# Interleaving the first two query passes by halves of the keys, and adding causal masks on TensorE instead of selecting on GpSimd, in a two-part attention kernel

## Chip, cores, metric

One core of one Trainium2 chip. The metric is the device time of one execution in microseconds, as the median of several executions. Below, PE is TensorE, ACT is ScalarE, DVE is VectorE, POOL is GpSimd. All runs compared here are of the fast state. One profile is one execution.

## The reference, cut to what matters

```python
def _A_ref(x, wqkv, wo):                      # S = 2048, D = 448, H = 16, Dh = 28
    ...
    scores = jnp.einsum('bhqd,bhkd->bhqk', q, k) * Dh ** (-0.5)
    p = _softmax(scores, axis=-1)             # full attention, no mask
    o = jnp.einsum('bhqk,bhkd->bhqd', p, v)
    ...
def _B_ref(x, wq, wk, wv, wo, beta):          # four segments of 512, causal within each
    ...
    for s in range(N):
        logits = jnp.einsum('bhqd,bhkd->bhqk', qs, ks) * scale + mask
        p = _softmax(logits, axis=-1)
        a_dot = jnp.einsum('bhqk,bhkd->bhqd', p, vs)
        ... # plus a linear-attention memory of the segments before, mixed in by sigmoid(beta)
```

Part A has 1024 banks of scores (I call a bank the scores of 128 keys by 512 queries for one head). Part B, of which only the causal blocks are computed and packed, has 160.

## The kernel before

Each bank needs an exp. Most go through ACT, in units of alternately three and two banks, with one PSUM buffer for each size, so that PE can write the scores of one unit while ACT reads the other. Some banks of part A ("DVE banks") go through a polynomial exp on DVE instead. There the `fraction` step runs on POOL if POOL is free, else on DVE.

The instructions of every engine are issued in an order that the kernel's Python plans with a model of the engines' times (`m["dve"]`, `m["pool"]` and so on). The model decides how many banks go to DVE. It adds zero "filler" matmuls (`fill`) where PE's recent load is below a limit; in that load each matmul's columns count by the share of the array that its tile covers.

The causal masks of part B before the change, after the exp, on POOL, with what the model charges for them:

```python
def emit_scores():                            # cut
    ...                                       # scores of the unit's banks into ps (PE)
    nc.scalar.activation(out=pt[:, 0:n, :], in_=ps[:, 0:n, :], func=ACT.Exp, scale=scale)
    e = on_act(n * CW, True, e)
    eff.append(e)
    ...
    while offs:                               # the diagonal blocks of the unit
        ...
        nc.gpsimd.affine_select(out=blk, in_=blk, compare_op=ALU.is_ge, fill=0.0,
                                base=0, pattern=pat, channel_multiplier=-1)
        p0 = max(m["pool"], e + SEM)
        m["pool"] = p0 + 260 + k * P          # POOL is taken: a fraction may go to DVE
        masks.append((p0, m["pool"]))         # DVE is charged 0.8 of each overlap with this
        e = m["pool"] + 30
        offs = offs[k:]
    ...                                       # then the products with V may be issued
```

```python
# the DVE exp of two banks: the fraction step
if m["pool"] > got + POOLQ:
    step(got, 267 * n, lambda: fraction(nc.vector), after_z)
    return
fraction(nc.gpsimd)
p0 = max(m["pool"], got)
m["pool"] = p0 + 160 + n * 595
masks.append((p0, m["pool"]))
```

The kernel keeps three more banks in PSUM, the "ring", for projections, DVE banks and the accumulators of the products with V. An accumulator holds its slot for a whole query pass of one head group. Before the change pass after pass is done; the projections and transposes of all of part A's keys for the first head group come ahead of everything else, and DVE takes no bank until they are nearly done.

The softmax here doesn't subtract the row's maximum and nothing guards it: scores larger than these inputs give would overflow.

Of the kernel before, what the change touches and what calls it, by code (L numbers as in the profile page):

```python
# [10 lines left out]
ALU = mybir.AluOpType  # L11
# [49 lines left out]
LASTV = 18  # L61
POOLQ = 300
HOLD = 0


@with_exitstack
def kernel(
# [126 lines left out]
        mblk.append(t)  # L194
    macc = const.tile([P, G, P], FP32)

    blocks = const.tile([P, P], BF16)
    nc.gpsimd.memset(blocks[:], 0.0)
    for j in range(4):
# [77 lines left out]
    def mm(out, mode, tl, n, dep, **kw):  # L277
        rows, cols = kw["lhsT"].shape[0], kw["lhsT"].shape[1]
        e = pe_time(mode, tl, n, dep, rows * cols / (P * P))
        nc.tensor.matmul(out, **kw)  # L280
        return e
# [15 lines left out]
    def dve(ready, prio, stream, emit, then=None, gate=None, slot=None):  # L297
        seq[0] += 1
        tasks.append((ready + SEM, prio, seq[0], stream, emit, then, gate, slot))
# [21 lines left out]
    for n, (kind, a, b) in enumerate(SEQ):  # L321
        T[kind, a, b] = len(order)
        if kind == "A":
            order += [("A", a, b, kt, j) for kt in range(NT) for j in range(4)]
        else:
            order += [(bk, b, s, None, j) for bk, s in (
                ("X", 2 * a), ("Y", 2 * a), ("Z", 2 * a), ("X", 2 * a + 1), ("Y", 2 * a + 1))
                for j in range(4)]
    T_END = len(order)
    ends = [T[k] for k in SEQ[1:]] + [T_END]  # L330

# [11 lines left out]
    def diag_blocks(b):  # L343
        return {"A": [], "X": [0], "Y": [0, 3 * P], "Z": [0, 2 * P]}[b[0]]
# [53 lines left out]
    unit_left = []  # L398
    unit_pv = []
    eff = []  # L400
    st = {"u": 0, "pos": 0, "ys": 0, "es": 0, "work": 0.0, "nrm": 0, "ot": 0}
    taken = set()


# [133 lines left out]
    def emit_scores():  # L538
        u = st["u"]
        bs, pos = next_banks()  # L540
        nb = NBS[u % 2]
        dep = max(when([x for b in bs for x in score_toks(b)]), eff[u - 2] if u >= 2 else 0.0)
        ps = scp.tile([P, nb, CW], FP32, tag=f"sc{nb}", name="ps_s")
        e = 0.0
        parts = [(n, i, b, p_) for i, b in enumerate(bs) for n, p_ in enumerate(score_parts(b))]
        for n, i, b, (t, q0, o0, w) in sorted(parts, key=lambda x: x[0]):
            kind, g, s, kt, j = b
            side = "A" if kind == "A" else "B"
            rows = slice(j * HP, j * HP + DH)
            kk, qq = kT[side, g, t // 4], qT[side, g, q0 // CW]  # L550
            for x in kq_of(b, t, q0):
                kq_used(x)
            ko, qo = t % 4 * P, q0 % CW
            e = max(e, mm(ps[:, i, o0:o0 + w], "S", j, w, dep,
                          lhsT=kk[rows, ko:ko + P], rhs=qq[rows, qo:qo + w],
                          start=True, stop=True, tile_position=(j * HP, 0)))
        n = len(bs)
        if u >= 2 * PT_BUFS:
            e = max(e, unit_pv[u - 2 * PT_BUFS])
        pt = ptp.tile([P, nb, CW], BF16, tag=f"pt{nb}", name="pt")  # L560
        nc.scalar.activation(out=pt[:, 0:n, :], in_=ps[:, 0:n, :], func=ACT.Exp, scale=scale)  # L561
        e = on_act(n * CW, True, e)
        eff.append(e)
        ptf = pt[:].rearrange("p n c -> p (n c)")
        offs = [i * CW + o for i, b in enumerate(bs) for o in diag_blocks(b)]
        while offs:
            k = 1
            if len(offs) > 1:
                step = offs[1] - offs[0]
                while k < len(offs) and offs[k] - offs[k - 1] == step:  # L570
                    k += 1
            if k == 1:
                blk, pat = ptf[:, offs[0]:offs[0] + P], [[1, P]]
            else:
                base = ptf[:, offs[0]:offs[0] + P]
                blk = bass.AP(tensor=base.tensor, offset=base.offset,
                              ap=[base.ap[0], [step, k], [1, P]])
                pat = [[0, k], [1, P]]
            nc.gpsimd.affine_select(out=blk, in_=blk, compare_op=ALU.is_ge, fill=0.0,  # L579
                                    base=0, pattern=pat, channel_multiplier=-1)  # L580
            p0 = max(m["pool"], e + SEM)
            m["pool"] = p0 + 260 + k * P
            masks.append((p0, m["pool"]))
            e = m["pool"] + 30
            offs = offs[k:]
        unit_left.append(sum(len(pv_parts(b)) for b in bs))
        unit_pv.append(0.0)
        for i, b in enumerate(bs):
            for part in pv_parts(b):
                pend.append([e, b, i, pt, part, u])  # L590
        st["u"] += 1
        st["pos"] = pos
        return bs
# [418 lines left out]
    def t_piece(r, half):  # L1012
        box = {}

        def atom(i, t0):
            def f(slot, dep):
                if i == 0 and t0 == 0:
                    box["ps"] = ring([P, 2, CW], BF16, "ps_t", slot)
                c = 2 * half + i
                for t in (t0, t0 + 1):  # L1020
                    e = pe_time("F", 0, P, dep)
                    nc.tensor.transpose(box["ps"][:, i, t * P:(t + 1) * P],  # L1022
                                        xnA[r][:, t, XC[c]:XC[c] + P], ident[:])
                return e
            return f

        def evac(e, slot):
            def then(e):
                slots[slot] = e
                rt["x", "A", r, half] = e  # L1030
            dve(e, 0, 533, lambda: nc.vector.tensor_copy(
                out=xT(slice(2 * half, 2 * half + 2), r * CW, (r + 1) * CW),
                in_=box["ps"][:]), then)

        return piece(0, [("xn", r)], [("F", 114, atom(i, t0)) for i in range(2) for t0 in (0, 2)],
                     evac)
# [175 lines left out]
    def spread(items, p0, p1):  # L1212
        cost = [sum(a[1] for a in it["atoms"]) + 100 for it in items]
        tot, c = sum(cost), 0.0
        for it, k in zip(items, cost):
            it["pos"] = p0 + (p1 - p0) * c / tot
            plan.append(it)
            c += k

    def q_(side, g, sc):  # L1220
        return kq_piece("q", side, g, sc)

    def k_(side, g, sc):
        return kq_piece("k", side, g, sc)

    head = [kq_piece("k", "A", 0, 0, P, 2 * P), kq_piece("k", "A", 0, 0, 2 * P, CW),
            t_piece(1, 0), t_piece(1, 1), k_("A", 0, 1),
            v_piece("A", (0, 1), 0), v_piece("A", (2, 3), 0),
            t_piece(2, 0), t_piece(2, 1), k_("A", 0, 2),
            v_piece("A", (4, 5), 0), v_piece("A", (6, 7), 0),  # L1230
            t_piece(3, 0), t_piece(3, 1), k_("A", 0, 3)]
    head += [v_piece("A", (t, t + 1), 0) for t in range(8, 16, 2)] + [q_("A", 0, 1)]
    spread(head, -100, -50)

    first = [q_("A", 0, 2), k_("A", 1, 0), q_("A", 1, 0), k_("A", 1, 1), q_("A", 1, 1),
             k_("A", 1, 2), q_("A", 1, 2), q_("A", 0, 3), k_("A", 1, 3), q_("A", 1, 3)]
# [128 lines left out]
    def fuse(bs):  # L1365
        used = {b[4] for b in bs}
        if sum(x["pos"] < 0 for x in side_work) > HEADQ:
            return
        for _ in range(2):
            if backlog(m["top"]) > BACKLOG:  # L1370
                return
            s = free_slot(m["top"])
            if s is None:
                return
            b = vbank_pick(used)
            if b is None:
                return
            emit_vbank(b, s)
            used.add(b[4])
# [42 lines left out]
    def pe_step(t):  # L1422
# [5 lines left out]
        if bs:  # L1428
            r = when([x for b in bs for x in score_toks(b)])
            if r is None:  # L1430
                force = "side"
            elif u >= 2 * PT_BUFS and unit_left[u - 2 * PT_BUFS]:
                force = "pv"
            else:
                avail = max(r, eff[u - 2] if u >= 2 else 0.0) + SEM
                deadline = m["act"] - 435
                if avail <= t + 4:
                    got = emit_scores()
                    fuse(got)
                    return  # L1440
        elif not ended and not side_work and not plan and not open_ and not tasks_left():
            fs = [i for i in range(3) if slots[i] is not None]
            if len(fs) >= 2:
                last_step(3, fs[0])
                last_step(2, fs[1])
                last_begin()
                ended.append(1)
                return
# [105 lines left out]
```

## Time and profile before

| | before |
|---|---|
| time | 510.46 us (510.23 to 510.75) |
| banks on DVE, of 1184 | 130 |
| units of three and two banks on ACT | 211 and 210, and one of a single bank |
| first exp starts, last exp ends, end | 8.3, 497.9, 508.4 us |
| DVE idle from 10 to 40 us | 15.6 us |
| DVE idle from 210 to 430 us (part B is spread over this) | 22.6 us |

The first lines of the page: the busy time of each engine, then the same in 40 slices of 12.7 us, in tenths; PEclk is the clock that TensorE was granted.

```profile
span 508.4 us, 12361 instructions
...
PE 475.4 (94%) x4918; PEld 168.6 (33%) x4918; DVE 445.7 (88%) x777; ACT 492.9 (97%) x450; POOL 144.6 (28%) x199
...
DVE  4349999999999999989989989879979958998993
...
POOL 8202211221122110351260431372161183202110
PEclk9999999999999999999999999999999999999999
```

ACT is busy wherever there is anything to do. DVE is not: its row begins with 4349, and from the 18th slice on it has sevens and eights. The costliest groups (line, engine, operation, tiles, shape and count; busy us and mean ns; idle before, and what ended it):

```profile
L561 ACT ACTIVATE pt<-ps_s 128x1536 bf16<-128x1536 f32 (+1 forms) x422 | 480.4, 1337 | 2.0 <-PE ps_s L280 1.3
...
L513 POOL TENSOR_SCALAR vz<-vy 128x1024 f16<-128x1024 uint16 x59 | 71.0, 1203 | 290.6 <-DVE vy L458 147.0
...
L579 POOL TENSOR_SCALAR_AFFINE_SELECT pt<-pt 128x256 bf16<-128x256 bf16 (+3 forms) x112 | 59.5, 559 | 54.4 <-ACT pt L561 54.3
L280 PE MATMUL acc<-warm 128*32 128x512 bf16 (+1 forms) x634 | 68.5, 384 | 0.0
```

The 112 selects take 59.5 us of POOL, the fillers 68.5 us of PE. Put in order of time, two exps start never closer than 1.330 us (three banks) or 0.903 us (two banks). I call "late starts" the sum of what the distances between consecutive exps have above that: 7.5 us. A bank on ACT therefore costs (1.330 + 0.903) / 5 = 0.447 us, and ACT leaves nothing else to gain than banks moved away, late starts and the two ends.

Two stretches of 25 us with part B in them (from and to in us, its length, then busy us and instructions of PE, PE's weight loads, DVE, ACT, POOL, then clock, DMA share and GB/s):

```profile
325.00:350.00 25.00, 22.75 (x291) 8.68 (x283) 19.76 (x41) 24.60 (x24) 16.28 (x29) 1.00 0.16 41
400.00:425.00 25.00, 22.64 (x255) 8.50 (x248) 18.29 (x37) 24.40 (x23) 15.21 (x29) 1.00 0.17 48
```

DVE has 5 to 7 us of idle in each, POOL is busy for over 15 us.

### The profile page before, as it was taken

What the parts mean: (1) busy time and instruction counts of PE and PEld (TensorE: products, weight loads), DVE (VectorE), ACT (ScalarE), POOL (GpSimd) and SP (SyncE); (2) the same over time, 40 slices, a digit from 0 to 9 for tenths busy, and PEclk for the clock granted to TensorE, in tenths of its full rate; (3) what the DMA queues carried; (4) which work ended last, traced back from release to release, by engine and by line L of the source; (5) the groups of instructions that cost most, each with busy time, mean ns of one, the idle gap of its engine ahead of it and who ended that gap; (6) DMA issues with size and microseconds to landing.
All of it is one profiled execution on the core that took longest, in us unless ns stands there. A gap on an engine that the chain in (4) does not pass through costs nothing.

```text
span 508.4 us, 12361 instructions
## 1 busy us (share of the span) xinstructions
PE 475.4 (94%) x4918; PEld 168.6 (33%) x4918; DVE 445.7 (88%) x777; ACT 492.9 (97%) x450; POOL 144.6 (28%) x199
## 2 busy tenths in 40 slices
PE   8999999999999999999889999899999999999996
PEld 5443233343332333333223333433333333333332
DVE  4349999999999999989989989879979958998993
ACT  5999999999999999999999999999999999999993
POOL 8202211221122110351260431372161183202110
PEclk9999999999999999999999999999999999999999
DMA  9200000000033100022021102012312120312112
GB/s 249 56 1 5 22 13 13 3 22 4 23 109 73 37 9 3 23 66 48 20 66 46 44 6 65 23 31 65 101 52 57 50 76 18 108 50 60 39 48 65
DMA packets 42178, 23.76 MB, mean 47 GB/s; under 512 B 22636, under 2 KB 37804, under 8 KB 42120
## 3 DMA queue, kind: packets, MB, share of 16 engines
q1 hardware_dynamic: 40808, 21.72, 16.1%
q0 software_dynamic: 416, 0.81, 0.7%
q8 instruction: 38, 0.62, 0.5%
q10 hardware_dynamic: 896, 0.45, 0.3%
q14 instruction: 20, 0.16, 0.1%
HBM read 16.58 MB, written 4.28 MB: 41 GB/s over the span
## 4 chain that ended last, share of the span: by engine, by line
ACT 52%; PE 22%; issue 19%; DVE 5%; POOL 1%; DMA 1%; DVEq 0%; ACTq 0%; POOLq 0%
ACT pt L561 50%; PE ps_s L280 6%; PE acc L280 5%; PE ps_proj L280 3%; PE ps_v L280 2%; PE ps_y L280 2%; ACT phiq L1042 1%; PE ps_kn L280 1%; PE ps_warm L219 1%; DVE vy L458 1%; DVE y L1080 1%; POOL pt L579 1%; DVE vz L505 1%; DVE oT L753 1%; PE ps_t L1022 0%
## 5 line engine op out<-in xcount | busy, mean ns | idle before, releaser
L561 ACT ACTIVATE pt<-ps_s 128x1536 bf16<-128x1536 f32 (+1 forms) x422 | 480.4, 1337 | 2.0 <-PE ps_s L280 1.3
L280 PE MATMUL ps_s<-qTA,kTA 28*128 28x512 bf16 x894 | 141.1, 383 | 20.3 <-ACT pt L561 17.4
L513 POOL TENSOR_SCALAR vz<-vy 128x1024 f16<-128x1024 uint16 x59 | 71.0, 1203 | 290.6 <-DVE vy L458 147.0
L280 PE MATMUL acc<-pt,vA 128*32 128x512 bf16 x894 | 116.8, 386 | 0.0
L280 PEld LDWEIGHTS <-kTA 28*128 28x128 bf16 x1024 | 46.4, 91 | 144.1 <-issue 140.0
L495 DVE SCALAR_TENSOR_TENSOR ve<-vy,vz 128x1024 uint16<-128x1024 int32 x65 | 80.8, 1243 | 0.1
L579 POOL TENSOR_SCALAR_AFFINE_SELECT pt<-pt 128x256 bf16<-128x256 bf16 (+3 forms) x112 | 59.5, 559 | 54.4 <-ACT pt L561 54.3
L280 PE MATMUL acc<-warm 128*32 128x512 bf16 (+1 forms) x634 | 68.5, 384 | 0.0
L506 DVE TENSOR_TENSOR vz<-vz,vl 128x1024 f16<-128x1024 f16 x65 | 50.1, 770 | 0.1
L280 PEld LDWEIGHTS <-vA 128*32 128x32 bf16 x1024 | 31.7, 94 | 47.8 <-issue 41.1
L505 DVE TENSOR_TENSOR vz<-vz 128x1024 f16<-128x1024 f16 x65 | 47.2, 726 | 0.2
L280 PE MATMUL ps_proj<-xT_100,wst 128*32 128x512 bf16 x512 | 38.3, 383 | 0.1
L280 PE MATMUL ps_proj<-xT_99,wst 128*32 128x512 bf16 (+2 forms) x512 | 37.1, 374 | 0.3 <-DVE vy L458 0.2
L280 PE MATMUL acc<-ve,vA 128*32 128x512 bf16 x130 | 33.5, 383 | 0.0
L280 PEld LDWEIGHTS <-wst 128*32 128x32 bf16 x1024 | 22.4, 95 | 28.2 <-issue 18.4
L280 PE MATMUL ps_s<-qTB,kTB 28*128 28x384 bf16 (+3 forms) x256 | 25.7, 299 | 5.0 <-ACT pt L561 4.2
L509 DVE TENSOR_SCALAR vl<-vz 128x1024 f16<-128x1024 f16 x65 | 27.3, 420 | 1.2 <-POOL vz L513 1.2
L720 DVE COPY osb<-acc 128x512 f32<-128x512 f32 x31 | 21.2, 683 | 7.0 <-PE acc L280 7.0
L280 PEld LDWEIGHTS <-warm 128*32 128x32 bf16 (+1 forms) x642 | 18.9, 94 | 21.5 <-issue 15.3
L753 DVE TENSOR_TENSOR oT<-osb,bc 128x512 bf16<-128x512 f32 x31 | 24.7, 797 | 0.0
L280 PE MATMUL acc<-pt,vB 128*32 128x128 bf16 (+3 forms) x256 | 20.5, 303 | 0.6 <-POOL pt L579 0.4
L280 PE MATMUL ps_y<-woB,oT 128*128 128x448 bf16 x80 | 20.7, 356 | 0.2
(388 smaller groups left out, 496.9 us busy)
## 6 DMA issues: line engine op xcount, KB each, us to landing
out_dram<-y SPq DMA_DIRECT2D x31, 112.0 KB
xn<-in_A_x_dram SPq DMA_DIRECT2D x3, 448.0 KB
wst<-in_A_wqkv_dram SPq DMA_DIRECT2D x2, 249.0 KB
woA<-in_A_wo_dram POOLq DMA_DIRECT2D x4, 98.0 KB, 7.2
woB<-in_B_wo_dram POOLq DMA_DIRECT2D x4, 98.0 KB, 4.5
wst<-in_A_wqkv_dram SPq DMA_DIRECT2D x1, 336.0 KB
wst<-in_B_wv_dram SPq DMA_DIRECT2D x1, 336.0 KB
wst<-in_B_wk_dram SPq DMA_DIRECT2D x1, 336.0 KB
```

What stands on the lines that cost most here:

```text
L219: nc.tensor.matmul(wps[:], lhsT=warm[:, 0:P], rhs=warm[:], start=True, stop=True)
L280: nc.tensor.matmul(out, **kw)
L458: dve(e0, 0, 533, lambda: nc.vector.tensor_scalar(out=pr["y"][:, i, :], in0=ps[:], scalar1=Y1, scalar2=Y0, op0=ALU.mult, op1=ALU.add), aft ...
L495: step(t, 533 * n, lambda: nc.vector.scalar_tensor_tensor(out=ef.bitcast(U16), in0=y, scalar=2.0 ** -9, in1=z, op0=ALU.mult, op1=ALU.add), ...
L505: step(t, 267 * n, lambda: nc.vector.tensor_mul(z, z, z), lambda t: step(t, 267 * n, lambda: nc.vector.tensor_mul(z, z, l), whole))
L506: lambda t: step(t, 267 * n, lambda: nc.vector.tensor_mul(z, z, l), whole))
L509: step(t, 133 * n, lambda: nc.vector.tensor_scalar(out=l, in0=z, scalar1=Z3, scalar2=Z2, op0=ALU.mult, op1=ALU.add), square)
L513: eng.tensor_scalar(out=z, in0=y.bitcast(U16).rearrange("p (c t) -> p c t", t=2)[:, :, 0], scalar1=2.0 ** -16, scalar2=Z0, op0=ALU.mult, o ...
L561: nc.scalar.activation(out=pt[:, 0:n, :], in_=ps[:, 0:n, :], func=ACT.Exp, scale=scale)
L579: nc.gpsimd.affine_select(out=blk, in_=blk, compare_op=ALU.is_ge, fill=0.0, base=0, pattern=pat, channel_multiplier=-1)
L720: nc.vector.tensor_copy(out=os_[0][:], in_=a[:])
L753: nc.vector.tensor_mul(get_oT(side, s)[:, g, :], os_[0][:], bc[:])
```

## The change

It has two parts. First, the order of the first two query passes is changed to first half of the keys for pass 0, first half for pass 1, second halves for both; half of the first projections can then come later, and DVE may take banks early. Second, the masks become matmuls: a triangle of -1e9 times the identity is to be added to the diagonal blocks of the scores in PSUM, before the exp, and the selects go, together with what the model charged for them.

```diff
+triu = const.tile([P, P], BF16)              # -1e9 where masked, built once on POOL
 ...
+first = order[:128]
+half = [[b for b in first if b[2] == cq and (b[3] < SPLIT) == lo] for cq in range(2)
+        for lo in (True, False)]
+order[:128] = half[0] + half[2] + half[1] + half[3]
 ...                                          # in emit_scores, after the scores:
+fuse(bs)                                     # DVE banks of this round, moved up to here
+for i, b in enumerate(bs):
+    offs = diag_blocks(b)
+    ...
+    e = max(e, mm(blk, "F", 0, k * P, 0.0, lhsT=ident[:], rhs=tri, start=False,
+                  stop=True, skip_group_check=True))
 ...                                          # after the exp:
-while offs:
-    ...
-    nc.gpsimd.affine_select(out=blk, in_=blk, ...)
-    p0 = max(m["pool"], e + SEM)
-    m["pool"] = p0 + 260 + k * P
-    masks.append((p0, m["pool"]))
-    e = m["pool"] + 30
 ...
-st = {..., "ys": 0, ...}                     # DVE's input buffers, shared with part A's x
+st = {..., "ys": 3, ...}                     # ... each counted free once its x is transposed
 ...
-head = [k, k, t(1), t(1), k1, v, v, t(2), t(2), k2, v, v, t(3), t(3), k3, v, v, v, v, q1]
+head = [k, k, t(1), t(1), v, k1, v, q1, v, v]                  # before anything else
+head = [t(2), t(2), k2, t(3), t(3), v, k3, v, v, v]            # spread over banks 8 to 72
 ...                                          # scores with masks are planned earlier:
-deadline = m["act"] - 435
+k = sum(len(diag_blocks(b)) for b in bs)
+deadline = m["act"] - 435 - (k and SWITCH + k * P / 2.4 + MLEAD)
```

(The head lists are abbreviated.)

More of the change, by code (lines that the diff above doesn't have):

```diff
@@ L63 @@
 HOLD = 0
+MLEAD = 0
+SPLIT = 8
 @with_exitstack
@@ L195 @@
     macc = const.tile([P, G, P], FP32)
+    triu = const.tile([P, P], BF16)
+    nc.gpsimd.memset(triu[:], 0.0)
+    nc.gpsimd.affine_select(out=triu[:], in_=triu[:], compare_op=ALU.is_ge, fill=-1e9,
+                            base=0, pattern=[[1, P]], channel_multiplier=-1)
     blocks = const.tile([P, P], BF16)
@@ L400 @@
     eff = []
-    st = {"u": 0, "pos": 0, "ys": 0, "es": 0, "work": 0.0, "nrm": 0, "ot": 0}
+    st = {"u": 0, "pos": 0, "ys": 3, "es": 0, "work": 0.0, "nrm": 0, "ot": 0}
     taken = set()
@@ L556, in emit_scores @@
                           start=True, stop=True, tile_position=(j * HP, 0)))
+        fuse(bs)
+        for i, b in enumerate(bs):
+            offs = diag_blocks(b)
+            if not offs:
+                continue
+            k = len(offs)
+            blk = ps[:, i, 0:P]
+            if k > 1:
+                blk = bass.AP(tensor=blk.tensor, offset=blk.offset,
+                              ap=[blk.ap[0], [offs[1], 2], [1, P]])
+            tri = triu[:] if k == 1 else bass.AP(
+                tensor=triu[:].tensor, offset=triu[:].offset,
+                ap=[triu[:].ap[0], [0, 2], [1, P]])
+            e = max(e, mm(blk, "F", 0, k * P, 0.0, lhsT=ident[:], rhs=tri, start=False,
+                          stop=True, skip_group_check=True))
         n = len(bs)
@@ L564, in emit_scores @@
         ptf = pt[:].rearrange("p n c -> p (n c)")
-        offs = [i * CW + o for i, b in enumerate(bs) for o in diag_blocks(b)]
-        while offs:
-            k = 1
-            if len(offs) > 1:
-                step = offs[1] - offs[0]
-                while k < len(offs) and offs[k] - offs[k - 1] == step:
-                    k += 1
-            if k == 1:
-                blk, pat = ptf[:, offs[0]:offs[0] + P], [[1, P]]
-            else:
-                base = ptf[:, offs[0]:offs[0] + P]
-                blk = bass.AP(tensor=base.tensor, offset=base.offset,
-                              ap=[base.ap[0], [step, k], [1, P]])
-                pat = [[0, k], [1, P]]
-            nc.gpsimd.affine_select(out=blk, in_=blk, compare_op=ALU.is_ge, fill=0.0,
-                                    base=0, pattern=pat, channel_multiplier=-1)
-            p0 = max(m["pool"], e + SEM)
-            m["pool"] = p0 + 260 + k * P
-            masks.append((p0, m["pool"]))
-            e = m["pool"] + 30
-            offs = offs[k:]
         unit_left.append(sum(len(pv_parts(b)) for b in bs))
@@ L1030, in then @@
                 rt["x", "A", r, half] = e
+                st["ys"] -= half
             dve(e, 0, 533, lambda: nc.vector.tensor_copy(
@@ L1226 @@
     head = [kq_piece("k", "A", 0, 0, P, 2 * P), kq_piece("k", "A", 0, 0, 2 * P, CW),
-            t_piece(1, 0), t_piece(1, 1), k_("A", 0, 1),
-            v_piece("A", (0, 1), 0), v_piece("A", (2, 3), 0),
-            t_piece(2, 0), t_piece(2, 1), k_("A", 0, 2),
-            v_piece("A", (4, 5), 0), v_piece("A", (6, 7), 0),
-            t_piece(3, 0), t_piece(3, 1), k_("A", 0, 3)]
-    head += [v_piece("A", (t, t + 1), 0) for t in range(8, 16, 2)] + [q_("A", 0, 1)]
+            t_piece(1, 0), t_piece(1, 1), v_piece("A", (0, 1), 0), k_("A", 0, 1),
+            v_piece("A", (2, 3), 0), q_("A", 0, 1), v_piece("A", (4, 5), 0), v_piece("A", (6, 7), 0)]
     spread(head, -100, -50)
+    head = [t_piece(2, 0), t_piece(2, 1), k_("A", 0, 2), t_piece(3, 0), t_piece(3, 1)]
+    head += [v_piece("A", (8, 9), 0), k_("A", 0, 3)]
+    head += [v_piece("A", (t, t + 1), 0) for t in range(10, 16, 2)]
+    spread(head, 8, 8 * SPLIT + 8)
     first = [q_("A", 0, 2), k_("A", 1, 0), q_("A", 1, 0), k_("A", 1, 1), q_("A", 1, 1),
@@ L1435, in pe_step @@
                 avail = max(r, eff[u - 2] if u >= 2 else 0.0) + SEM
-                deadline = m["act"] - 435
+                k = sum(len(diag_blocks(b)) for b in bs)
+                deadline = m["act"] - 435 - (k and SWITCH + k * P / 2.4 + MLEAD)
                 if avail <= t + 4:
-                    got = emit_scores()
-                    fuse(got)
+                    emit_scores()
                     return
```

## The prediction

> **What bounds it now.** ScalarE (ACT): 97% busy by the page (492.9 of 508.4 us), 480.4 of it in 422 exps of scores. In order of time, two exps start never closer than 1.330 us (three banks of 512 scores) or 0.903 us (two banks); 211 and 210 of them make 470 us. The rest of 8.3 to 497.9 us is other activations (14 us) and about 7.5 us of stalls. The head before and the 10.5 us tail after stay as they are. So time moves only (a) by 0.447 us (2.233/5) for each bank that goes to DVE instead, and (b) by ACT stalls.
>
> DVE computes 130 of 1184 banks (count of its score reads). A bank costs it 0.69 + half of (1.24 + 0.77 + 0.73 + 0.42) = 2.27 us (groups by shape). DVE is 98% busy from 40 to 200 us, but idle about 16 us between 10 and 40 us, and about 20 us in the ten-us windows from 210 to 430 us that hold part B's selects.
>
> **What the change does.**
> 1. 112 selects on POOL, 59.5 us, go. POOL is hardly on the chain (1%); PE waited for selects 0.4 us in all. DVE instructions overlapped by selects lasted only some 2 us longer in total[...]. The larger effect is indirect: the model in the kernel that orders the emission charges DVE 0.8 of each overlap with a select and sends the fraction step to DVE when POOL is late (6 times, 0.74 us each). Without that, part B should use perhaps half its 20 us of idle DVE, plus 4.4 + 2 us: some 7 more banks, -3 us.
> 2. Interleaved halves: half of the first projections is deferred, and DVE banks may start near 20 instead of 36 us. But two live accumulators leave one of three PSUM ring slots for projections and DVE banks from about 23 to 52 us: only 3 or 4 more banks, -1.5 us, and 0.3 us fewer early stalls.
> 3. Mask matmuls: 160, of 128 or 256 columns, full-array mode. By the measured spacing (0.32 us for a 512-column group with a change of mode, against 0.21) a unit gets 0.1 us for the mode plus about 0.17 (two banks) or 0.26 us (three), between scores and exp. In part B's 34 three-bank units the last score now ends at a median 0.71 us after the previous exp's start, and that exp lasts 0.903: 0.36 us more doesn't fit. Two-bank units (1.330 us) fit. Scores can start somewhat earlier, so I charge 0.05 to 0.12 us per three-bank unit: +2 to +3.5 us. [...]
>
> **Sum.** 510.5 - 3 - 1.8 + 2.5 = about 508; the re-planned schedule may save a little more: 507.0 us, 8 in 10 between 502.5 and 511.5. Faster by over 2% 0.06, within 2% 0.91, slower 0.03.
>
> **What would show it.** DVE score reads 137 to 144; exps about 5 fewer; first DVE banks before 36 us. Median start-to-start of part B's three-bank units up from 0.903 to about 0.97 us. POOL busy down by about 60 us. ACT still at 96 to 97%.
>
> **What would make it wrong.** Projections starving behind one slot, so that ACT waits for keys at 35 to 50 us (slower); masks fully hidden, or 15 more DVE banks (502); masks stalling two-bank units too (512).

## The result, and the profile after

The change runs in 507.43 us (507.17 to 507.93, 4 runs) against 510.46 us. Ratios here are the mean time of one kernel's fast runs over that of the other's in the same rounds, so they are not quite the ratios of the medians. This one is 0.9941, 95% interval 0.9924 to 0.9959: 0.6% faster, within 2%.

The same lines of the page as before, then the same groups:

```profile
span 505.8 us, 12171 instructions
...
PE 474.5 (94%) x4877; PEld 170.7 (34%) x4883; DVE 466.0 (92%) x801; ACT 490.6 (97%) x446; POOL 104.2 (21%) x100
...
DVE  4779899999999999999999989999999999999992
...
POOL 8312211111132111111212111121111021112210
PEclk9999999999999999999999999999999999999999
```

```profile
L586 ACT ACTIVATE pt<-ps_s 128x1536 bf16<-128x1536 f32 (+1 forms) x418 | 477.4, 1300 | 1.9 <-PE ps_s L286 1.1
L523 POOL TENSOR_SCALAR vz<-vy 128x1024 f16<-128x1024 uint16 x70 | 89.4, 1278 | 379.9 <-DVE vy L468 223.3
...
L286 PE MATMUL acc<-warm 128*32 128x512 bf16 (+2 forms) x429 | 47.8, 383 | 0.2
...
L286 PE MATMUL ps_s<-triu,ident 128*128 128x256 bf16 (+1 forms) x160 | 25.7, 255 | 0.0
```

POOL is 40 us less busy (not 60: eleven more fractions run there). DVE's row begins 4779 and has hardly an eight left. There are 160 mask matmuls, 25.7 us of PE. PE isn't busier for them: the fillers went down from 68.5 to 47.8 us. The two stretches with part B again:

```profile
325.00:350.00 25.00, 22.62 (x275) 9.34 (x277) 23.47 (x47) 24.73 (x24) 5.41 (x4) 1.00 0.21 58
400.00:425.00 25.00, 21.69 (x261) 9.54 (x259) 24.44 (x52) 24.81 (x23) 3.60 (x3) 1.00 0.19 52
```

DVE is busy where it was idle, and POOL is down to a third and a quarter.

Where the 2.5 us between the two profiles' spans come from, in us (before rounding the spans are 508.35 and 505.83):

| piece | before | after | difference |
|---|---|---|---|
| start to first exp | 8.3 | 8.4 | +0.1 |
| least time of the exps (units of three x 1.330 + of two x 0.903) | 470.3 | 465.8 | -4.5 |
| late starts | 7.5 | 9.4 | +2.0 |
| other activations between, and the single bank | 11.9 | 12.1 | +0.2 |
| last exp to end | 10.4 | 10.1 | -0.3 |

DVE takes 140 banks in place of 130. By time of their score reads:

| banks on DVE that start in | 0 to 60 us | 60 to 200 | 200 to 430 | after |
|---|---|---|---|---|
| before | 11 | 46 | 53 | 20 |
| after | 14 | 46 | 62 | 18 |

The first starts at 15.9 us, where it was 36.9. DVE's idle time falls from 15.6 to 7.0 us between 10 and 40 us, and from 22.6 to 9.2 us between 210 and 430 us.

The masks can be seen on PE. These are a three-bank unit of part B (start us, us, instruction):

```profile
329.79 0.40 PE L286 MATMUL ps_s<-qTB,kTB 28*128 28x384 bf16 x6 [0.25 <-ACT pt L586]
330.12 0.50 PE L286 MATMUL ps_s<-triu,ident 128*128 128x256 bf16 x3
330.55 0.35 PE L286 MATMUL acc<-pt,vB 128*32 128x384 bf16 x4
```

Scores start at 329.79, the masks follow at 330.12 and end at 330.62, 0.83 us after the scores began. Over part B's 35 three-bank units the last of scores and masks ends at a median 0.935 us after the exp before started (0.712 us in the kernel before), and the exp starts at a median 1.032 us (0.903 before). The two-bank units, whose exp before takes 1.330 us, go from 1.330 to 1.348 us. Summed over part B's three-bank units that follow another exp directly, late starts rise from 1.8 to 4.2 us.

### The profile page after: what moved, and what is told of

It is laid out like the page before. It is cut to its first block, busy times and chain, and to the rows that moved or that the text cites. A ratio compares the mean times of both kernels' runs of the same rounds, so it can differ in the third digit from the quotient of the medians.

```text
span 505.8 us, 12171 instructions
## 1 busy us (share of the span) xinstructions
PE 474.5 (94%) x4877; PEld 170.7 (34%) x4883; DVE 466.0 (92%) x801; ACT 490.6 (97%) x446; POOL 104.2 (21%) x100
## 4 chain that ended last, share of the span: by engine, by line
ACT 54%; PE 22%; issue 19%; DVE 4%; ACTq 0%; DVEq 0%
ACT pt L586 53%; PE ps_s L286 7%; PE ps_proj L286 5%; PE acc L286 4%; PE ps_y L286 2%; ACT phiq L1047 1%; PE ps_v L286 1%; PE ps_warm L225 1%; DVE ve L505 0%; DVE vB L831 0%; DVE vy L468 0%; DVE vl L519 0%; DVE vz L516 0%; DVE vz L515 0%; ACT phik L867 0%
## 5 line engine op out<-in xcount | busy, mean ns | idle before, releaser
L523 POOL TENSOR_SCALAR vz<-vy 128x1024 f16<-128x1024 uint16 x70 | 89.4, 1278 | 379.9 <-DVE vy L468 223.3
L286 PE MATMUL acc<-pt,vA 128*32 128x512 bf16 x884 | 112.1, 386 | 0.0
L505 DVE SCALAR_TENSOR_TENSOR ve<-vy,vz 128x1024 uint16<-128x1024 int32 x70 | 88.4, 1262 | 0.3
L516 DVE TENSOR_TENSOR vz<-vz,vl 128x1024 f16<-128x1024 f16 x70 | 57.4, 820 | 0.5
L515 DVE TENSOR_TENSOR vz<-vz 128x1024 f16<-128x1024 f16 x70 | 52.5, 751 | 0.2
L286 PE MATMUL acc<-warm 128*32 128x512 bf16 (+2 forms) x429 | 47.8, 383 | 0.2
L286 PEld LDWEIGHTS <-wst 128*32 128x32 bf16 x1024 | 22.5, 95 | 26.3 <-issue 16.8
L286 PE MATMUL ps_s<-qTB,kTB 28*128 28x512 bf16 (+3 forms) x256 | 26.3, 299 | 5.5 <-ACT pt L586 3.8
L286 PE MATMUL ps_s<-triu,ident 128*128 128x256 bf16 (+1 forms) x160 | 25.7, 255 | 0.0
L757 DVE TENSOR_TENSOR oT<-osb,bc 128x512 bf16<-128x512 f32 x31 | 22.6, 730 | 0.0
L286 PE MATMUL ps_y<-woB,oT 128*128 128x448 bf16 x80 | 21.2, 356 | 0.0
L1085 DVE CAST y<-ps_y 128x448 bf16<-128x448 f32 x28 | 17.2, 619 | 1.9 <-PE ps_y L286 1.8
L286 PEld LDWEIGHTS <-warm 128*32 128x32 bf16 (+1 forms) x447 | 13.3, 94 | 15.5 <-issue 10.7
```

Source lines behind the costliest of these rows:

```text
L286: nc.tensor.matmul(out, **kw)
L505: step(t, 533 * n, lambda: nc.vector.scalar_tensor_tensor(out=ef.bitcast(U16), in0=y, scalar=2.0 ** -9, in1=z, op0=ALU.mult, op1=ALU.add), ...
L515: step(t, 267 * n, lambda: nc.vector.tensor_mul(z, z, z), lambda t: step(t, 267 * n, lambda: nc.vector.tensor_mul(z, z, l), whole))
L516: lambda t: step(t, 267 * n, lambda: nc.vector.tensor_mul(z, z, l), whole))
L523: eng.tensor_scalar(out=z, in0=y.bitcast(U16).rearrange("p (c t) -> p c t", t=2)[:, :, 0], scalar1=2.0 ** -16, scalar2=Z0, op0=ALU.mult, o ...
L757: nc.vector.tensor_mul(get_oT(side, s)[:, g, :], os_[0][:], bc[:])
```

## The experiments

The rows are in the order in which they ran, and times are medians. "Rest" is the time from the first exp's start to the last exp's end, less the least time of the exps that ran there: it holds some 12 us of other activations and all waiting of ACT. Clock is that of the profiled run. "Tail" is the time from the last exp to the end.

| run | us | ratio to before (95%) | banks on DVE | rest | tail | clock granted |
|---|---|---|---|---|---|---|
| before | 510.5 | | 130 | 19.4 | 10.4 | 1.00 |
| the change | 507.4 | 0.994 (0.992 to 0.996) | 140 | 21.5 | 10.1 | 1.00 |
| e1 interleaving only | 508.5 | 0.996 (0.995 to 0.998) | 131 | 19.0 | 9.5 | 1.00 |
| e2 masks only | 514.5 | 1.008 (1.006 to 1.009) | 136 | 23.2 | 13.7 | 0.99 |
| e3 selects stay, not charged | 519.4 | 1.019 (1.017 to 1.022) | 137 | 33.5 | 11.5 | 0.99 |
| e4 e3 with interleaving | 515.9 | 1.012 (1.009 to 1.014) | 139 | 28.0 | 11.0 | 0.99 |
| e5 change, no mask matmuls | 509.5 | 0.998 (0.997 to 0.999) | 140 | 22.5 | 10.1 | 0.97 |
| e6 e2 with another end | 513.1 | 1.006 (1.004 to 1.007) | 132 | 21.2 | 11.4 | 1.00 |
| e7 e1, DVE not charged | 509.6 | 0.999 (0.998 to 1.000) | 138 | 21.8 | 10.5 | 1.00 |
| e8 masks on PE for two-bank units | 513.4 | 1.006 (1.005 to 1.007) | 138 | 25.0 | 10.4 | 1.00 |
| e9 masks beside, 124 of 160 | 509.9 | 1.000 (0.998 to 1.001) | 140 | 23.8 | 10.1 | 0.98 |
| e10 change, another plan | 509.2 | 0.998 (0.997 to 0.999) | 138 | 21.9 | 10.6 | 1.00 |
| e11 masks only, another plan | 515.3 | 1.010 (1.008 to 1.011) | 138 | 27.7 | 11.8 | 0.99 |
| e12 masks beside, 149 of 160 | 513.0 | 1.004 (1.002 to 1.006) | 140 | 28.9 | 10.2 | 0.98 |

All passed the comparison with the reference. That includes e5, e9 and e12, which leave the causal mask out: this comparison can't see whether part B is masked at all, so it says nothing for or against the new masks.

The experiments ran on four chips, each beside the kernel before, whose medians there were 510.34 to 510.55 us.

One rival has to be kept in mind for every loss below: PE's clock. Leaving out the last 10 us, the profiles show half clock for 6.8 us in e2, 13.7 in e3, 10.2 in e4, 30.7 in e5, 3.4 in e8, 20.5 in e9, 6.8 in e11 and 23.9 in e12, and none in the kernel before, the change, e1, e6, e7 and e10. In e3 6.7 us of the late starts lie in these stretches. The clock isn't the whole loss there: three of e3's six runs had a mean clock of 1.00 and took 518.3 to 519.5 us, two of e11's took 514.8 and 515.1 us.

### Each part alone: e1 and e2

e1 is the kernel before with the order, the head lists and the buffer count of the change. e2 is the change with those put back.

> Only the interleaved halves (order, deferred projections, buffer count); selects stay on GpSimd as before. The plan has 132 banks on DVE, 2 more than before. Theory (a bank moved is worth 0.447 us of ScalarE, nothing else changes): -0.9 us, 509.6 us; ScalarE stalls and late starts stay near 7.5 us. Rival (interleaving is the main gain of the change): 508.5 us or less, by fewer stalls in the first 60 us.

> Only the masks on TensorE, with the score order of before. The plan has 136 banks on DVE, 6 more. Theory: 6 x 0.447 = -2.7 us from the banks, +2 us from three-bank units of part B waiting for their masks (median start to start about 1.03 us in place of 0.903): 509.8 us. Rival (masks hidden behind the running exp, the 2 us of late starts come from the new plan): 507.9 us.

e1 ran in 508.5 us, the rival's number, but not for the rival's reason: late starts were 7.3 us. DVE took 14 banks before 60 us, as in the change, but lost two at the end (131 in all; one pair held a single bank, so the plan's 132 was my miscount). In the profile the time from the first to the last exp fell by 0.4 us (the exp of a single bank went away) and the tail by 0.9 us. So the early banks are there, and part of the gain is an end that fell better.

e2 ran in 514.5 us, far above both numbers. The median start to start of part B's three-bank units was 1.028 us, as in the change, so the masks do what the theory said. But late starts were 11.6 us instead of 9.4 (1.8 of them in a stretch at half clock from 421 us on), and the tail 13.7 us instead of 10.1. The waits of ACT show the tail; first e2, then the change (who waited for whom: us, times, longest):

```profile
ACT osb L1198 <- PE acc L286: 5.7, 1, 5.7
```

```profile
ACT osb L1200 <- PE acc L286: 2.1, 1, 2.1
```

In e2 the final copy waits 5.7 us, because PE still has a row of output projections to issue whose PSUM slots DVE empties late. The parts alone give about -1.8 and +3.9 us, together -3.0: they don't add up.

### Is it the model's charge or the engine? e3, e4, e7

I had put the gain of the second part on the model: without the charge for selects it plans more DVE banks. Then the selects could stay on POOL, uncharged, and no mask would stand before an exp.

```diff
-p0 = max(m["pool"], e + SEM)                 # e3, e4
-m["pool"] = p0 + 260 + k * P
-masks.append((p0, m["pool"]))
-e = m["pool"] + 30
+e = max(e + SEM, st.get("sel", 0.0)) + 290 + k * P
+st["sel"] = e - 30
```

> The kernel before, selects still on GpSimd, no masks on TensorE and no interleaving; only the emission model no longer charges DVE and GpSimd for the selects (they still delay the readiness of the products). The plan has 138 banks on DVE, 8 more. Theory (the gain of taking selects off GpSimd is the plan's, not the engine's): 8 x 0.447 = -3.6 us, 506.9 us, with late starts still 7 to 8 us. Rival (GpSimd must really be free, else fractions come late and DVE is held up by the selects, so that the extra banks end in waits of ScalarE): 509 us or more, late starts up by 2 us or more.

> Interleaved halves as in the change, selects on GpSimd but not charged in the emission model. 140 banks on DVE, as many as the change has, and no masks between scores and exps. Theory: 10 x 0.447 = -4.5 us, no mask waits: 506.0 us, 1.5 to 2 us faster than the change. Rival (GpSimd must be free): no faster than the change, 507.5 us or more.

The theory fell. e3 got 137 banks onto DVE and was 8.8 us slower than the kernel before in the same rounds, with 21.9 us of late starts in its profile; e4 had 16.4. These are the selects of the kernel before and of e3, and what waited for them:

```profile
L579 POOL TENSOR_SCALAR_AFFINE_SELECT pt<-pt x112: 284/407/1666, 217.1 to 424.1; 128x256 bf16<-128x256 bf16 x66, 128x384 bf16<-128x384 bf16 x16, 128x128 bf16<-128x128 bf16 x16, 128x512 bf16<-128x512 bf16 x12
...
who waited for it (us, times):
  PE acc L280: 0.4, 1
```

```profile
L579 POOL TENSOR_SCALAR_AFFINE_SELECT pt<-pt x114: 288/546/1615, 216.7 to 434.1; 128x256 bf16<-128x256 bf16 x75, 128x128 bf16<-128x128 bf16 x15, 128x384 bf16<-128x384 bf16 x12, 128x512 bf16<-128x512 bf16 x7
...
who waited for it (us, times):
  PE acc L280: 4.4, 10
```

PE's waits for selects go from 0.4 to 4.4 us in all. The next scores stand behind such a wait in PE's order, and ACT behind them (e8 below shows one). But this is the smaller part: in e4 PE waits for selects only 0.4 us. PE's waits for DVE grow more, from 2.9 us in all before to 8.6 in e3 and 11.0 in e4, and so do DVE's waits for the fraction step on POOL (`vl` behind `vz`), from 1.2 to 4.5 and 6.9 us. POOL does selects and fractions in one order, and the plan took the selects' time there for free. From the waits of the kernel before, of e3, and of e4 (two lines):

```profile
DVE vl L509 <- POOL vz L513: 1.2, 1, 1.2
```

```profile
DVE vl L509 <- POOL vz L513: 4.5, 5, 1.9
```

```profile
DVE vl L514 <- POOL vz L518: 6.9, 9, 1.5
...
PE acc L281 <- POOL pt L584: 0.4, 2, 0.2
```

e7 keeps POOL's time in the model and drops only the charge on DVE (the line `masks.append`), on top of e1.

> Interleaved halves, selects on GpSimd with their GpSimd time counted in the emission model, but no charge on DVE for overlaps. 138 banks on DVE. Theory (e3 and e4 failed because GpSimd ran over in part B, where selects and fractions queue in order): late starts fall from e4's 16.4 to 9 us or less, 507 to 508 us. Rival (what hurts is DVE being slowed by selects): late starts stay above 13 us, 511 us or more.

Late starts fell to 9.9 us and the time to 509.6 us, between the two expectations. Counting POOL's time repairs most of the loss. But the seven banks that e7 has more than e1 bring nothing: e1 is 1.1 us faster. The charge of 0.8 on DVE, of which I saw almost nothing in DVE's own durations, seems worth having. (In e7 there is more to see: DVE's instructions that selects overlap take 6.2 us more in all than the medians of their kinds, before the change 2.0.)

### Why a fuller DVE hurts selects: e8

Three-bank units didn't hide their masks in the change (1.032 us from exp to exp against 0.903), two-bank units nearly did (1.348 against 1.330). So e8 puts only the latter on PE, and leaves the selects of the former on POOL, with POOL's time counted.

```diff
-offs = diag_blocks(b)                        # mask matmuls
+offs = diag_blocks(b) if nb == 2 else []
 ...                                          # after the exp, as in the kernel before:
+offs = [i * CW + o for i, b in enumerate(bs) for o in (diag_blocks(b) if nb == 3 else [])]
+    nc.gpsimd.affine_select(...)
+    p0 = max(m["pool"], e + SEM); m["pool"] = p0 + 260 + k * P; e = m["pool"] + 30
```

> The change, but masks on TensorE only for units of two banks (that follow an exp of 1.33 us and fit under it); three-bank units keep the select on GpSimd, with GpSimd's time counted and DVE not charged. 138 banks on DVE. Theory: part B's three-bank units back at a median near 0.904 us, late starts about 7.5 us, 506.5 us. Rival (half of the selects on GpSimd is already too much for it in part B): late starts above 10 us, 509 us or more.

It ran in 513.4 us, so the rival held. Three-bank units were back at a median of 0.904 us, as the theory has it, and yet ACT lost more than it won. This is the worst place (start us, us, instruction, with the engine's idle time before it and what ended that):

```profile
253.14 5.87 POOL L604 TENSOR_SCALAR_AFFINE_SELECT pt<-pt 128x384 bf16<-128x384 bf16 x4 [8.04 <-ACT pt L586]
...
255.40 0.54 PE L286 MATMUL acc<-pt,vB 128*32 128x512 bf16 x5 [0.39 <-POOL pt L604]
...
255.49 0.67 DVE L516 TENSOR_TENSOR vz<-vz,vl 128x1024 f16<-128x1024 f16 x1
...
256.09 0.67 DVE L523 TENSOR_SCALAR vz<-vy 128x1024 f16<-128x1024 uint16 x1
256.69 1.21 DVE L505 SCALAR_TENSOR_TENSOR ve<-vy,vz 128x1024 uint16<-128x1024 int32 x1
258.11 0.34 PE L286 MATMUL acc<-pt,vB 128*32 128x128 bf16 x3 [2.17 <-POOL pt L604]
...
258.88 1.45 ACT L586 ACTIVATE pt<-ps_s 128x1536 bf16<-128x1536 f32 x1 [2.20 <-PE ps_s L286]
```

The four selects from 253.14 us on take 5.87 us. The second of them, of 128x128 elements, starts at 255.31 us and takes 2.752 us. It is the longest in the summary of e8's selects (shortest, median and longest ns):

```profile
L604 POOL TENSOR_SCALAR_AFFINE_SELECT pt<-pt x64: 289/522/2752, 216.8 to 425.1; 128x256 bf16<-128x256 bf16 x36, 128x128 bf16<-128x128 bf16 x11, 128x384 bf16<-128x384 bf16 x9, 128x640 bf16<-128x640 bf16 x4
```

The shortest select of that shape takes 0.289 us, so this one is 9.5 times as long. During those 2.75 us DVE runs, back to back, a product of two SBUF tensors, a scaling, and another two-input instruction, at about their usual lengths (0.67, 0.67 and 1.21 us; the means in the kernel before are 0.77, 0.74 and 1.24). PE waits 2.17 us for that select, and ACT 2.20 us for the scores that PE holds behind it; from 259.2 us on PE then has half clock (0.50) for 3.4 us. Where selects overlapped with DVE's instructions, it was mostly the selects that took longer. Before the change the 112 selects lost 14.3 us (the sum of each one's length over the shortest of its shape), DVE's instructions that they overlapped only some 2 us. Of the 14.3 us, 11.1 belong to the 29 selects that met a DVE instruction with two inputs in SBUF; the 18 that met no DVE instruction lost 0.1 us.

So the idle time of DVE beside the selects wasn't only slack that a pessimistic model gave away: selects got through in it. With more banks there the selects were longer (they lose 27.6 us in e3 and 25.2 in e7, where it was 14.3), and a long select reached ACT through PE (2.17 us of PE's waiting and 2.20 of ACT's, above). That can't happen if the selects leave POOL. That is what the second part of the change is for. How much time this costs is less sure. In e7 the selects lost nearly as much as in e3, yet with POOL's time in the plan PE waited for them 1.9 us and late starts were 9.9 us. That they are what ate the 3.1 us of its seven extra banks (7 x 0.447) is argued, not shown; the other order in e10 alone is worth 0.8 us.

### What the masks cost where they stand: e5, e9, e12

e5 leaves the mask matmuls out but keeps their time in the model, so order and bank counts are those of the change.

```diff
-e = max(e, mm(blk, "F", 0, k * P, 0.0, lhsT=ident[:], rhs=tri, ...))
+e = max(e, pe_time("F", 0, k * P, 0.0))
```

> The change, same emission order and same bank counts, but the 160 mask matmuls are left out (the emission model still counts their time). The result is wrong on purpose: part B is not causal. Theory (the late starts come from the mask matmuls between scores and exps): late starts fall from 9.4 to about 7.3 us, part B's three-bank units go back from a median of 1.03 to 0.904 us, time 505.3 us. Rival (the late starts are of the order, not of the matmuls): 507 us, late starts above 9 us.

The units started on time (median 0.904 us), yet late starts were 9.9 us and it was 2.1 us slower than the change. TensorE had lost its clock. Two stretches of 3.4 us, e5 first, then the change (PE's busy us is the second number, the granted clock the one after POOL):

```profile
322.40:325.80 3.40, 2.63 (x38) 1.09 (x34) 3.15 (x5) 3.40 (x4) 1.42 (x1) 1.00 0.26 77
325.80:329.20 3.40, 2.97 (x23) 0.76 (x23) 3.40 (x11) 3.40 (x4) 1.16 (x1) 0.59 0.00 0
```

```profile
322.40:325.80 3.40, 3.26 (x44) 1.23 (x36) 3.26 (x6) 3.40 (x4) 0.90 (x1) 1.00 0.17 47
325.80:329.20 3.40, 3.02 (x40) 1.55 (x39) 3.29 (x9) 3.33 (x4) 0.87 (x2) 1.00 0.14 37
```

PE is busy for 2.63 of 3.40 us here, where the change has 3.26. Then the clock granted in e5 goes from 1.00 to 0.50 for some 15 us, and this twice in the execution; in the change, which differs by the mask matmuls alone, it stays at 1.00. Late starts in those stretches eat the gain. So the mask matmuls pay part of their price back: they stand in for fillers (68.5 us before, 47.8 in the change). In e5 nothing stood in for them, because its model went on counting the load of the absent masks: it issued as many fillers as the change (447 weight loads of zeros in both).

e9 and e12 try to keep PE busy: each mask matmul is replaced by one of its size that adds zeros to an open accumulator (e9), or else writes to a free ring slot (e12), so that no exp waits for it.

> As e5, the result wrong on purpose, but where an accumulator is open each mask matmul is replaced by one of the same size that adds zeros to it, so that TensorE stays as busy and only the exp no longer waits. Theory (e5 lost its gain because TensorE, less busy, was granted a lower clock, 0.97): clock back to 0.99 or more, late starts about 7 us, 505.5 us; so the masks cost about 2 us where they stand. Rival (the mask's wait costs nothing, or e5 was slow for another reason): 507 us or more at a clock of 0.99 or more.

> As e9, but where no accumulator is open the substitute writes to a free PSUM slot, so that 149 of the 160 mask matmuls (e9: 124) have a substitute that no exp waits for. Wrong result on purpose. Theory (e9 lost only to half clock from 407 us on, where its substitutes were missing): clock 0.99 or more in the whole run, late starts about 7.5 us, 505.5 us: the price of the masks' place, about 2 us. Rival (zeros do not keep the clock up as masks do, or order and not waiting decides): clock below 0.99, or 507 us or more at full clock.

Neither kept the clock: 0.98 both times, and both were slower than the change. From 406 us on, first e9, then e12, then the change:

```profile
406.20:409.60 3.40, 2.31 (x35) 1.09 (x34) 3.40 (x9) 3.40 (x4) 1.05 (x1) 0.73 0.05 8
409.60:413.00 3.40, 2.65 (x26) 0.58 (x22) 3.40 (x9) 2.90 (x4) 0.00 (x0) 0.50 0.28 81
```

```profile
406.20:409.60 3.40, 3.01 (x29) 1.24 (x24) 3.40 (x8) 3.40 (x4) 1.23 (x1) 1.00 0.02 5
409.60:413.00 3.40, 2.87 (x33) 1.01 (x32) 3.40 (x9) 3.35 (x4) 1.04 (x1) 0.81 0.28 75
413.00:416.40 3.40, 3.23 (x27) 0.77 (x25) 2.43 (x6) 2.45 (x3) 0.00 (x0) 0.50 0.18 41
```

```profile
406.20:409.60 3.40, 2.61 (x32) 1.47 (x29) 3.40 (x9) 3.37 (x4) 1.50 (x1) 1.00 0.01 2
409.60:413.00 3.40, 2.82 (x36) 1.38 (x37) 3.40 (x8) 3.40 (x3) 1.05 (x1) 1.00 0.28 76
```

In e9 PE had little to do when the clock fell (2.31 of 3.40 us), as in e5. In e12 it had more, by busy time: 3.01 and 2.87 us against 2.61 and 2.82 us in the change, which keeps full clock. So busy time alone doesn't tell these cases apart. I tried an estimate from the traces instead. In each of them the changes of the clock lie whole multiples of 3.413 us apart (501.76 us, 147 times that, in the change's and in that of the kernel before), so I cut each trace into windows of that length, with the changes on their borders. In each I sum the columns of PE's matmuls, each times the share of 128x128, the largest tile in the traces, that its tile covers, as `fill` does, over the columns that the window has room for (512 in 0.216 us, the spacing of projections at full clock). This estimate of mine is 0.22 to 0.35 in the window before each of the twelve falls that come before the last 10 us (0.34 in e12, with PE busy for 2.79 of 3.41 us) and never under 0.37 in the change between 20 and 490 us. It doesn't separate the cases cleanly: of 1880 windows of all traces at whose end full clock stayed, ten are under 0.36 (one is in the kernel before, 0.33 from 407.8 us on). Why the clock fell is not shown. Whether the zeros in the substitutes matter besides is open. e12 has a further fault of its own: between 325 and 350 us, at full clock, its late starts are 1.7 us, where the change has 0.8; I didn't follow up where they come from.

What is left is the stretch from 200 to 325 us, in which all these runs had full clock, and which holds three of the eight passes of part B. Late starts there were 2.7 us in the change and 1.5, 1.9 and 1.8 us in e5, e9 and e12. So the place of the masks costs 0.8 to 1.2 us in three passes; for eight, if they are alike, I estimate 2 to 3 us. This agrees with the 2.4 us by which late starts of part B's three-bank units rise from the kernel before to the change (1.8 to 4.2 us). No run shows the whole price at full clock.

### How much is the plan's luck: e6, e10, e11

e6 is e2 with one number changed for the last query pass alone, so that the order is the same up to there.

```diff
-if i == n and len(free) < LASTV:
+if i == n and len(free) < (LASTV if i < len(SEQ) - 1 else 40):
```

> Masks only (as e2), with one number changed for the last query pass alone: DVE takes no bank when fewer than 40 (before: 18) are left. The order is the same until the last pass; 132 banks on DVE, 4 fewer. Theory (most of what e2 lost against the change is its end: 5.7 us from the last exp to the final copy, because DVE is late with its last banks and output copies): the gap falls to about 2 us, ScalarE gets 1.8 us more of exps, 512.7 us. Rival (e2 lost its time earlier): the gap stays at 5 us or more, or 514.5 us or more.

513.1 us, with a wait of 3.4 us before the final copy instead of 5.7 us and a tail of 11.4 us. The theory holds for the tail, at a price of four banks; the end of e2 was over-filled. It explains at most half of e2's distance from the change. Part of the 1.4 us may also be clock: e6's profile has full clock where e2's, in the same order, loses it at 421 us.

e10 and e11 move one constant of the plan by 30 ns (MLEAD = 30), in the change and in e2.

> The change with one planning constant moved: scores with masks are planned 30 ns earlier. 138 banks on DVE. The same instructions per bank in another order. Theory (the order alone is worth little): 508.3 us, 0.9 more than the change for two banks fewer. Rival (the plan by chance moves a few us, so that e2's loss and the change's gain are both partly chance): 510 us or more.

> Masks only (as e2), with the same constant moved by 30 ns. 138 banks on DVE, two more than e2. Theory (masks without interleaving lose at their end and in late starts whatever the order): 513 to 515 us. Rival (chance of the plan): 510.5 us or less.

e10 ran in 509.2 us: two banks fewer are 0.9 us, and 0.8 us are the other order. e11 ran in 515.3 us: it has two banks more than e2, but one hole of over 4 us at 400 us, where ACT stands behind an activation whose query projection comes late. So a plan may move by a microsecond or more through nothing but its order. The lead of the change over both e2 and e11, 7 to 8 us, is more than that, so masks without interleaving seem to plan badly in a systematic way; why an interleaved start helps the order at 400 us is not settled.

No version that I ran beats the change.

## Why the prediction was right

The time (507.43 us against 507.0) and the range were right, and most terms were near. That the centre fell within half a microsecond is luck: the terms summed to 508, and e10 shows that 30 ns in the plan move the time by 1.7 us, two banks included. One of its reasons was wrong.

1. What bounds the kernel: right (DVE from 40 to 200 us is 97% busy by the trace, not 98%). ACT is busy 97% of the span before and after, and the gain is banks moved (-4.5 us for ten) less late starts (+2.0 us).
2. Selects to masks, "some 7 more banks, -3 us": the size is right (nine more between 200 and 430 us, of which two are given back at the end), the reason half wrong. The step that failed is "the larger effect is indirect: the model in the kernel that orders the emission". The model's charge did hold banks back, but it held them back for a cause. Take the charge away and leave the selects, and the kernel is 8.8 us slower (e3). With GpSimd's time counted and only DVE's charge gone (e7), seven more banks than in e1 gain nothing. Of my runs, those with more than a bank or two extra were faster than e1 only in the change, where the selects are off GpSimd. I looked for the price of the overlap in the durations of DVE's instructions (2 us) and not in those of the selects, which were up to 1.67 us long, with a median of 0.41.
3. Interleaving, "3 or 4 more banks, -1.5 us": three banks more before 60 us, in the change and in e1. DVE's idle time between 10 and 40 us fell by 8.6 us. That the third ring slot is what limits it was argued from the code and not tested.
4. Masks before the exps, "+2 to +3.5 us": right, late starts of part B's three-bank units rose by 2.4 us. They start at a median of 1.032 us, where I said about 0.97, so the median is 0.13 us later and not 0.05 to 0.12. That the total is no larger has two causes: these units had stalls of 1.8 us before, which the 4.2 us after take in, and the two-bank units nearly hid their masks (1.348 us against 1.330), as predicted. From the start of the scores, of 512 columns per tile, to the start of the masks it is a median 0.326 us. Groups of 512 columns that follow one another with the same tile shape are 0.216 us apart. The difference, 0.11 us, comes with the change of mode; 0.1 us was predicted.
5. What I left out: the mask matmuls displace fillers, so PE is no busier than before (474.5 us against 475.4), and the clock that TensorE was granted differed between runs that differ in PE's work in part B alone: 1.00 in the change, 0.97 in e5, 0.98 in e9 and e12. In the profiles of eight of my twelve experiments TensorE lost it for 3.4 to 30.7 us.

One caution on the change itself. In 96 of part B's 160 banks there are two score groups, and the second group's matmul is issued with `start=True` before the mask. Whether the mask is then added to the first group's diagonal scores, as it should be, was not tested: no run here shows it, and the comparison, which doesn't see a missing mask, wouldn't.

## What to carry to other kernels

Idle time of one engine beside work of another may be what that work needs, as here, where the 18 selects beside an idle DVE lost 0.1 us and 29 beside DVE instructions with two inputs 11.1: before filling it, look at the durations of both engines' instructions, not only of the one that you want to fill. A matmul that replaces work of another engine may also do something for TensorE's clock: with the masks it was 1.00 here, without them 0.97 (e5). If you take work from TensorE to measure its cost, look at the granted clock before you believe the time. In a kernel whose order is planned, a part of a change can be slower alone than the whole, so test parts, but also the plan's own scatter.
